# Reordering engine instructions in the first two wide attention pairs of a fused attention and ELU-FFN kernel

## The chip, the cores and the metric

The kernel runs on one core of a Trainium2 chip. The metric is the time of one execution on the device in microseconds (us). Before the change it is 1258.76 us, the median of 3 runs (1257.75 to 1259.64).

## The reference

Two blocks follow each other. The attention block keeps only scores close to the row maximum; the second block is a two-layer FFN with an ELU between the layers. Everything is float32.

```python
# q, k, v: (8, 8, 576, 64), batch x heads x sequence x head size; tau = 0.02
scores = 1/sqrt(64) * q @ k.transpose(0, 1, 3, 2)
thresh = max(scores, axis=-1) - tau
scores = where(scores >= thresh, scores, -1e9)
attn = exp(scores - max(scores)); attn = attn / (sum(attn) + 1e-9)
x = (attn @ v).transpose(0, 2, 1, 3).reshape(4608, 512)
h = x @ w_in                                   # (512, 2048)
g = where(h > 0, h, exp(min(h, 0)) - 1)
out = g @ w_out                                # (2048, 512)
```

## The kernel before, in words

Attention goes by pairs of heads, 32 in all, numbered from 0. A pair has four square query steps (128 queries of both heads) and one tail step (the last 64 queries of both). A step is: score matmuls into PSUM, a row maximum on VectorE (DVE), an exponential on ScalarE (ACT), a mask with row sums on DVE, a scaling on GpSimd (POOL) or ACT, and a turn: DVE transposes 32x32 blocks into a tile `x` (`turn_squares`, L868 and L877), SyncE (SP) stores `x` to DRAM (`there`, L881 for a tail step, L893 for a square one), and a later DMA brings it back turned. There are two buffers of `x`, so a turn can begin only when the stores of the turn before the last one have landed.

From pair 9 on (`JOINED`) the pairs are wide: two square steps share five PSUM banks. `tail_step` issues the tail scores of the own pair and the value matmuls of an older pair, `wide_step` the scores of two square steps, and between them TensorE (PE) gets quarters of FFN work: Strassen products of the first layer (`first_product`) and of the second (`second_round`). One `first_product` has seven quarters, which go through three PSUM banks in turn:

- quarter 0 ends in an ACT copy `w1`, 1 in an ACT copy `u2` and a POOL addition `u2 += w1`, 2 in an ACT copy `s1` and a POOL subtraction `s1 -= u2` (copies L1692, POOL L1697);
- quarters 3 and 4 end in an ACT copy into the hidden tile `g` (L1739, L1740), 4 also in a POOL subtraction `t5` (L1697);
- quarters 5 and 6 end in a DVE addition out of PSUM into `g` (L1700, with operand `t5` or `s1`), and then in an ELU: ACT exponential (L1708), minus one on ACT (L1720) or POOL (L1718), DVE combination (L1728).

The bank of a quarter is free for a quarter of the next product once its copy or addition has been done.

Every engine runs its own instructions in order. The order is planned on the host: `at(t, f, key)` puts a job on an agenda with due time `t` plus an offset `MOVED[stage + key]`, and jobs are issued by due time whenever the planned PE clock passes them. The stage is `j` in pair 9 and `s` or `f` in later pairs, so an offset whose name begins with `j` acts in pair 9 alone. The key `5.0` is job 0 behind quarter 5 of the pair (28 quarters, four products); `max30` is the maximum of step 3, head 0; `exp30`, `exp31` are its exponentials; `turn4` is the turn of the tail step; `w0` stores 512 KB of weight sums to DRAM (L2097).

```python
        def at(t, f, key=None):
            if key and stage[0]:
                t += MOVED.get(stage[0] + key, 0.0)
```

Accesses to the five wide banks go through `on_banks`: any engine's access to a bank waits for all earlier accesses of other engines to that bank, reads included. An exponential of step 3 thus waits for a maximum issued before it on a shared bank.

In `tail_step` of pair 10, the values of pair 8 are copied out of PSUM by ACT (`values_out`, L1060 and L1066) in a job that was due at the end of the value matmuls.

Of the kernel before, what the change touches and what calls it, by code (L numbers as in the profile page):

```python
# [368 lines left out]
def kernel(  # L369
# [545 lines left out]
    def values(pr, part, pv=None):  # L915
        b, j = divmod(pr, NPAIR)
        vm, vd = (raws[pr][x] for x in ("vm", "vd"))
        wT = wTs.pop((pr, part))
        if b not in xts:
            xts[b] = xpool.tile([P, KJ, MAIN], FP32, name="xt")  # L920
        n = wT.shape[1] * T
        if pv is None:
            pv = psum["t"].tile([P, 512], FP32, name="pv", tag="rt")
        watch = on_banks if wide else lambda *a: None
        watch(nc.tensor.matmul(pv[:, :n], vd, wT[:, :, NC], start=True, stop=False, skip_group_check=True), pv[:, :n])
        for c in range(NC):
            for h in range(2):
                g0, g1 = (2 * h, 2 * h + 10) if part else (0, 2 * NT)
                o = pv[h * D : (h + 1) * D, g0 * T : g1 * T]
                watch(nc.tensor.matmul(o, vm[:, h, c], wT[:, g0:g1, h * (NC + 1) + c], start=False, stop=(c == NC - 1),  # L930
                                       skip_group_check=True), o)
        return lambda: values_out(pr, part, pv)
# [49 lines left out]
    def wide_max(pr, i, h):  # L982
        st = open_steps[pr, i]
        on_banks(nc.vector.tensor_reduce(st["mx"][:, h : h + 1], st["sc", h], axis=AX.XY if i == NC else AX.X, op=ALU.max,  # L984
                                         negate=True),
                 st["sc", h])

    def wide_bounds(pr, i):
        st, hs = open_steps[pr, i], heads_of(i)
        sunk = [(pr, i, h) in WIDE_ACT for h in hs]  # L990
        for h in hs[:1] if len(set(sunk)) == 1 else hs:
            cs = slice(0, len(hs)) if len(set(sunk)) == 1 else slice(h, h + 1)
            if sunk[h]:
                nc.gpsimd.tensor_scalar(st["th"][:, cs], st["mx"][:, cs], ntau, None, ALU.subtract)
            else:
                nc.gpsimd.tensor_scalar(st["th"][:, cs], st["mx"][:, cs], -1.0, ntau, ALU.mult, ALU.add)  # L996

    def wide_exp(pr, i, h):
        st = open_steps[pr, i]
        if (pr, i, h) in WIDE_ACT:  # L1000
            on_banks(nc.scalar.activation(st["e", h], st["sc", h], AF.Prelu, bias=st["th"][:, h : h + 1], scale=1.0, alpha=STEEP),
                     st["sc", h])
        else:
            on_banks(nc.scalar.activation(st["e", h], st["sc", h], AF.Exp, bias=st["mx"][:, h : h + 1]), st["sc", h])  # L1004

    def wide_mask(pr, i, h):
        st = open_steps[pr, i]
        if (pr, i, h) in WIDE_ACT:
            nc.scalar.activation(st["e", h], st["e", h], AF.Exp, bias=ntau, accum_out=st["sm"][:, h, :1])
            return  # L1010
        on_banks(nc.vector.scalar_tensor_tensor(st["e", h], st["sc", h], st["th"][:, h : h + 1], st["e", h], ALU.is_ge,  # L1011
                                                ALU.mult, accum_out=st["sm"][:, h, :1]), st["sc", h])
# [602 lines left out]
    with tc.manual_schedule():  # L1615
# [14 lines left out]
            serial[0] += 1  # L1630
            heapq.heappush(agenda, (t, serial[0], f))
# [9 lines left out]
        def on_pe(cost, f):  # L1641
            until(clock[0])
            f()
            clock[0] += cost
            return clock[0]
# [261 lines left out]
        def finish_of(pr, i, t_sum, t_turn):  # L1907
            at(t_sum, lambda: reciprocal_of(pr, i, heads_of(i)), f"sum{i}")
            for h in heads_of(i):
                at(t_sum + 0.25 + 0.75 * h, lambda h=h: (normalize_act if (pr, i, h) in WIDE_NORM else normalize_pool)(pr, i, h), f"norm{i}{h}")  # L1910
            at(t_turn, lambda: turn_squares(pr, i), f"turn{i}")
# [6 lines left out]
        def tail_step(pr):  # L1918
            t, v = clock[0], pr - 2
            own, joined = pr if pr < NP else None, v if v >= JOINED else None  # L1920
            loc = {}
            on_pe(1.2, lambda: loc.update(zip(("main", "outs"), tails_and_values(own, joined))))
            if pr == JOINED:
                end = on_pe(2.5, lambda: loc.update(out=values(JOINED - 1, 0, wide[0][:, 2 * 512 : 3 * 512])))
                at(end - 2.0, lambda: loc["out"]())
            if own is not None:
                at(t + 1.25, lambda: wide_max(pr, NC, 0), "max4")
                at(t + 2.0, lambda: wide_bounds(pr, NC), "bound4")
                at(t + 2.0, lambda: wide_exp(pr, NC, 0), "exp4")
                at(t + 3.3, lambda: wide_mask(pr, NC, 0), "mask4")  # L1930
                finish_of(pr, NC, t + 4.2, t + 10.5)
            if joined is not None:
                for part, cost in ((1, 2.2), (0, 1.8)):
                    end = on_pe(cost, lambda: loc["main"](part))
                    at(end, loc["outs"][part], f"out{part}")
            elif v == JOINED - 1:
                end = on_pe(3.0, lambda: loc.update(out=values(v, 1, wide[0][:, 2 * 512 : 3 * 512])))
                at(end, lambda: loc["out"]())

        def wide_step(pr, half):  # L1940
            t = clock[0]
# [145 lines left out]
        for pr in range(JOINED, NP + 2):  # L2087
# [17 lines left out]
            if JOINED < pr < NP:  # L2105
                at(t + 7.0, lambda pr=pr: load(pr, ("v",)), "v" if stage[0] == "j" else None)
            tail_step(pr)
            v_end = clock[0]
            if pr % NPAIR == 1 and pr < NP + 1:
# [139 lines left out]
        end = middle + UNIT * NFT  # L2249
# [102 lines left out]
```

## Time and profile before

| | |
|---|---|
| median of 3 runs | 1258.76 us |
| the profiled execution | 1259.32 us |
| its span, first to last instruction | 1257.5 us |
| PE busy | 1243.9 us (99%) |
| DVE busy | 1040.3 us (83%) |
| POOL busy | 727.1 us (58%) |
| ACT busy | 635.2 us (51%) |
| DMA queue of SP | 72.2% of 16 engines' span |
| TensorE clock granted | 1.000 |

Pair 9 stands in the span from 259 to 293 us, the tail step of pair 10 from 293 to 300.5 us. In the timeline a row has its start in us, its length in us, the engine, the line, the operation, output and inputs, the shapes and a count; in brackets the idle time of the engine before it and what ended that.

### The profile page before, as it was taken

How to read it: one execution, taken by the hardware profiler on the slowest of the kernel's cores; microseconds unless marked ns; L12 is line 12 of the kernel's file. 1: busy time of each engine (PE TensorE's matmuls, PEld its weight loads, DVE VectorE, ACT ScalarE, POOL GpSimd, SP SyncE). 2: the span in 40 equal slices, each digit the busy share in tenths (PEclk: the TensorE clock that was granted, in tenths of full speed). 3: DMA queues.
4: the chain of work that ended last, by engine and by line, in shares of the span. 5: the costliest groups of instructions: out<-in, count | busy, mean ns of one | idle time of the engine just before them, and what ended most of it. 6: DMA issues, size and time to landing. Idle time of an engine off the chain costs nothing.

```text
span 1257.5 us, 21116 instructions
## 1 busy us (share of the span) xinstructions
PE 1243.9 (99%) x6598; PEld 957.0 (76%) x6598; DVE 1040.3 (83%) x2199; ACT 635.2 (51%) x1331; POOL 727.1 (58%) x1061
## 2 busy tenths in 40 slices
PE   8999999999999999999999999999999999999998
PEld 6676576467878787888778787878788887788886
DVE  7888778789798988898889879898889876776983
ACT  7989776664352526253534435252625353465330
POOL 4778655687475847666576747584766655122000
PEclk9999999999999999999999999999999999999999
DMA  7557688998889898998989998999889885000001
GB/s 134 151 177 177 177 244 234 260 248 216 239 239 266 245 240 224 241 263 228 252 206 253 237 231 231 256 257 240 228 238 262 221 241 175 20 1 1 1 34 34
DMA packets 325551, 245.74 MB, mean 195 GB/s; under 512 B 209216, under 2 KB 289984, under 8 KB 325440
## 3 DMA queue, kind: packets, MB, share of 16 engines
q1 hardware_dynamic: 323264, 243.65, 72.2%
q8 instruction: 52, 0.85, 0.3%
q10 hardware_dynamic: 2176, 0.75, 0.2%
q14 instruction: 59, 0.48, 0.1%
HBM read 154.53 MB, written 89.78 MB: 194 GB/s over the span
## 4 chain that ended last, share of the span: by engine, by line
PE 90%; DVE 3%; DMA 2%; ACT 2%; issue 1%; SPq 1%; POOL 1%; DVEq 0%; ACTq 0%; POOLq 0%
PE f L1678 23%; PE f L1818 22%; PE sc L977 8%; PE sc L1050 7%; PE f L2278 7%; PE f L2203 5%; PE f L1102 4%; PE sc L673 3%; PE f L1154 3%; PE f L2216 2%; PE pv L930 2%; PE rt L792 1%; PE sc L1042 1%; PE sc L1037 1%; DMA there<-x 1%
## 5 line engine op out<-in xcount | busy, mean ns | idle before, releaser
L984 DVE TENSOR_REDUCE mx<-sc 128x1 f32<-128x576 f32 x207 | 148.3, 750 | 28.5 <-PE sc L977 24.6
L726 POOL TENSOR_SCALAR w<-w,rs 128x576 f32<-128x576 f32 x144 | 115.8, 813 | 70.0 <-DVE rs L789 69.8
L1004 ACT ACTIVATE w<-sc,mx 128x576 f32<-128x576 f32 x113 | 81.5, 740 | 116.0 <-DVE mx L984 98.7
L868 DVE STREAM_TRANSPOSE x<-w 128x512 f32<-128x512 f32 (+1 forms) x153 | 108.9, 744 | 15.3 <-POOL w L726 11.3
L996 POOL TENSOR_SCALAR th<-mx,ntau 128x2 f32<-128x2 f32 (+1 forms) x114 | 33.8, 297 | 133.3 <-DVE mx L984 133.3
L977 PE MATMUL sc<-kT,qT 64*128 64x448 f32 (+4 forms) x736 | 103.4, 416 | 0.2 <-ACT xs L1066 0.2
L977 PEld LDWEIGHTS sc<-kT,qT 64*128 64x128 f32 x736 | 81.0, 186 | 25.1 <-issue 16.5
L1011 DVE SCALAR_TENSOR_TENSOR w<-sc,th,w 128x576 f32<-128x576 f32 x113 | 88.2, 811 | 9.4 <-ACT w L1004 9.2
L1678 PE MATMUL f<-xt,sw 128*128 128x256 f32 x384 | 93.8, 386 | 1.8 <-DVE g L1700 1.8
L1678 PE MATMUL f<-xt,w_in 128*128 128x256 f32 x384 | 92.2, 382 | 0.0
L1818 PE MATMUL f<-w_out,s 128*128 128x256 f32 x384 | 92.0, 382 | 0.1
L1818 PE MATMUL f<-w_out,g 128*128 128x256 f32 x384 | 92.0, 382 | 0.0
L1678 PE MATMUL f<-x,w_in 128*128 128x256 f32 x384 | 90.9, 379 | 0.0
L1818 PE MATMUL f<-t,s 128*128 128x256 f32 x384 | 90.8, 379 | 0.0
L726 POOL TENSOR_SCALAR e<-e,rs 128x576 f32<-128x576 f32 x91 | 67.1, 741 | 35.6 <-DVE rs L789 34.2
L1678 PEld LDWEIGHTS f<-xt,sw 128*128 128x128 f32 x384 | 69.4, 189 | 18.6 <-issue 4.8
L1678 PEld LDWEIGHTS f<-xt,w_in 128*128 128x128 f32 x384 | 71.7, 190 | 12.7 <-ACT w L1692 2.2
L1818 PEld LDWEIGHTS f<-w_out,g 128*128 128x128 f32 x384 | 72.0, 190 | 12.4 <-issue 3.1
L1818 PEld LDWEIGHTS f<-w_out,s 128*128 128x128 f32 x384 | 71.9, 190 | 12.4 <-issue 2.5
L1678 PEld LDWEIGHTS f<-x,w_in 128*128 128x128 f32 x384 | 72.8, 190 | 10.5 <-ACT s L1692 0.6
L1818 PEld LDWEIGHTS f<-t,s 128*128 128x128 f32 x384 | 72.8, 190 | 10.3 <-POOL s L1765 0.4
L1765 POOL TENSOR_TENSOR s<-g 128x256 f32<-128x256 f32 x96 | 74.9, 785 | 7.9 <-DVE g L1728 7.5
(316 smaller groups left out, 3103.5 us busy)
## 6 DMA issues: line engine op xcount, KB each, us to landing
there<-x SPq DMA_DIRECT2D x444, 144.0 KB, 3.5
wTb<-there SPq DMA_DIRECT2D x58, 576.0 KB, 6.5
wTa<-there SPq DMA_DIRECT2D x53, 576.0 KB, 5.0
sw<-win_sums SPq DMA_DIRECT2D x46, 384.0 KB, 4.9
t<-wout_sums SPq DMA_DIRECT2D x33, 512.0 KB, 6.2
qm<-in_q_dram SPq DMA_DIRECT2D x124, 72.0 KB, 4.9
wst<-in_moe_w_in_dram SPq DMA_DIRECT2D x16, 512.0 KB, 4.4
vm<-in_v_dram SPq DMA_DIRECT2D x64, 128.0 KB, 3.9
```

The lines of the kernel that those rows point to most:

```text
L726: nc.gpsimd.tensor_scalar(wv, wv, st["rs"][:, h : h + 1], 1.0, ALU.mult, ALU.mult)
L868: nc.vector.transpose(x[:, :, c0 : c0 + nc_], src.rearrange("p (c g n) -> p g c n", c=nc_, n=T))
L977: on_banks(nc.tensor.matmul(o, qT[r, i * P : (i + 1) * P], kT[r, k0 : k0 + n], start=True, stop=True, skip_group_check=True), o)
L984: on_banks(nc.vector.tensor_reduce(st["mx"][:, h : h + 1], st["sc", h], axis=AX.XY if i == NC else AX.X, op=ALU.max, negate=True), st["sc" ...
L1004: on_banks(nc.scalar.activation(st["e", h], st["sc", h], AF.Exp, bias=st["mx"][:, h : h + 1]), st["sc", h])
L1011: on_banks(nc.vector.scalar_tensor_tensor(st["e", h], st["sc", h], st["th"][:, h : h + 1], st["e", h], ALU.is_ge, ALU.mult, accum_out=st[" ...
L1050: on_banks(nc.tensor.matmul(o, vm[:, h, c], parts[part][:, g0:g1, h * (NC + 1) + c], start=False, stop=(c == NC - 1), skip_group_check=Tru ...
L1678: nc.tensor.matmul(loc["banks"][place], left[:, j], right[:, j], start=(begins and j == 0), stop=(j == 1), skip_group_check=True)
L1765: engine.tensor_tensor(o, x, y, op)
L1818: nc.tensor.matmul(place(m), lhs, rhs, start=(begins and v == 0), stop=(v == RU - 1), skip_group_check=True)
L2203: nc.tensor.matmul(o, w.rearrange("p (j f) -> p j f", j=KJ)[:, j], m, start=(j == 0 and x == 0), stop=(j == KJ - 1 and x == 1), skip_group ...
L2278: nc.tensor.matmul(banks8[2 * i + x // 2], h[:, tok], w, start=(f == 0 and x != 1), stop=(f == NFT - 1 and x != 0), skip_group_check=True)
```

## The change

Eight offsets and one due time change. No instruction is added or taken away; only the order on the engines is another. By the planned due times of the program:

- `turn4` goes from 10.84 to 12.44: on DVE it comes behind the additions of quarters 5 and 6 (11.07, 11.39) and the maximum `max10` (12.21); on SP its four stores come behind `w0` (11.90).
- `15.1` (`u2 += w1`) goes from 21.80 to 21.30, on POOL ahead of the thresholds of step 2 (21.58); `16.1` (`s1 -= u2`) goes from 23.17 to 24.37, so that `t5` of quarter 18 (23.78) comes ahead of it.
- `max30` goes from 23.54 to 25.44, on DVE behind the additions of quarters 19 and 20; `exp31` (24.20 to 25.60) and `exp30` (24.85 to 25.75) follow it as before. `19.0` goes from 25.16 to 24.76.
- `19.1` (an ELU's exponential) goes from 26.41 to 27.31, on ACT behind the copy `u2` of quarter 22.
- The copies of pair 8's values in pair 10's tail step are due 2.0 earlier, on ACT ahead of the exponential of pair 10's tail (`exp4`).

```diff
-    "j14.0": -3.68, "j15.0": -1.62, "j15.1": -0.67, "j16.0": 0.04, "j16.1": -0.22, "j16.2": 0.31, "j17.0": -2.16,
-    "j18.0": -0.97, "j19.0": -0.84, "j19.1": -0.29, "j18.1": -1.3, "j2.0": -4.57, "j2.1": 0.76, "j2.2": 0.93, "j20.0": -4.05, "j20.1":
+    "j14.0": -3.68, "j15.0": -1.62, "j15.1": -1.17, "j16.0": 0.04, "j16.1": 0.98, "j16.2": 0.31, "j17.0": -2.16,
+    "j18.0": -0.97, "j19.0": -1.24, "j19.1": 0.61, "j18.1": -1.3, "j2.0": -4.57, "j2.1": 0.76, "j2.2": 0.93, "j20.0": -4.05, "j20.1":
...
     "jexp00": -0.08, "jexp01": -0.52, "jexp10": -0.11, "jexp11": 0.42, "jexp20": -0.3, "jexp21": 0.68, "jexp30":
-    -0.93, "jexp31": -0.68, "jexp4": 0.88, "jfetch0": 2.01, "jfetch1": 4.84, "jloadk": -2.59, "jloadq": -4.91, "jm00":
+    -0.03, "jexp31": 0.72, "jexp4": 0.88, "jfetch0": 2.01, "jfetch1": 4.84, "jloadk": -2.59, "jloadq": -4.91, "jm00":
...
-    0.48, "jmax30": 1.11, "jmax31": 0.34, "jmax4": -9.77, "jnorm00": 0.93, "jnorm01": 0.48, "jnorm10": 0.12,
+    0.48, "jmax30": 3.01, "jmax31": 0.34, "jmax4": -9.77, "jnorm00": 0.93, "jnorm01": 0.48, "jnorm10": 0.12,
...
-    0.07, "jsum4": -0.37, "jturn0": -1.09, "jturn1": -0.06, "jturn2": 2.17, "jturn3": 0.29, "jturn4": -2.27, "jw0":
+    0.07, "jsum4": -0.37, "jturn0": -1.09, "jturn1": -0.06, "jturn2": 2.17, "jturn3": 0.29, "jturn4": -0.67, "jw0":
...
             elif v == JOINED - 1:
                 end = on_pe(3.0, lambda: loc.update(out=values(v, 1, wide[0][:, 2 * 512 : 3 * 512])))
-                at(end, lambda: loc["out"]())
+                at(end - 2.0, lambda: loc["out"]())
```

## The prediction, made before the changed kernel was run

> **What bounds the kernel now.** I read the page first, then the idle time of PE stretch by stretch, then the timelines of DVE, SP and ACT where PE idles.
>
> ```profile
> PE 1243.9 (99%) x6598; PEld 957.0 (76%) x6598; DVE 1040.3 (83%) x2199; ACT 635.2 (51%) x1331; POOL 727.1 (58%) x1061
> ```
>
> PE is the bound: 13.6 us of the span are idle. From 301 us on its timeline shows no wait that is not repeated in every pair, so a microsecond won or lost by then is won or lost at the end. The waits within reach stand in PE's own timeline:
>
> ```profile
> 268.93 1.03 PE L1678 MATMUL f<-xt,sw 128*128 128x256 f32 x4
> 271.32 1.13 PE L1678 MATMUL f<-xt,sw 128*128 128x256 f32 x4 [1.37 <-DVE g L1700]
> ...
> 287.23 1.13 PE L1678 MATMUL f<-xt,sw 128*128 128x256 f32 x4 [0.44 <-DVE g L1700]
> ...
> 297.14 1.02 PE L977 MATMUL sc<-kT,qT 64*128 64x448 f32 x2
> 298.40 2.17 PE L977 MATMUL sc<-kT,qT 64*128 64x320 f32 x14 [0.25 <-ACT xs L1066]
> ```
>
> Quarters follow each other at 0.87 us (two take 1.73 at 267.20 to 268.93). By that pitch the first wait costs 1.53 us, the second 0.61, the third about 0.6. All else between 263 and 301 us is 0.2 or less. These are what the change goes for; at most some 2.8 us can come back.
>
> **The first wait: additions ahead of the tail's turn.** DVE's timeline:
>
> ```profile
> 265.82 1.42 DVE L984 TENSOR_REDUCE mx<-sc 128x1 f32<-128x576 f32 x2
> 269.86 0.71 DVE L868 STREAM_TRANSPOSE x<-w 128x512 f32<-128x512 f32 x1 [2.62 <-DMA there<-x]
> 270.49 0.46 DVE L877 STREAM_TRANSPOSE x<-w 128x128 f32<-128x128 f32 x2
> 270.88 0.39 DVE L1700 TENSOR_TENSOR g<-f,t 128x256 f32<-128x256 f32 x1
> 271.19 0.41 DVE L1700 TENSOR_TENSOR g<-f,s 128x256 f32<-128x256 f32 x1
> ```
>
> DVE stands idle for 2.62 us at the tail's turn, for its tile `x`, and both additions queue behind it. Put ahead, the first can start when POOL's `t` ends (267.89 + 0.74 = 268.63), the second when quarter 6 ends (269.09). PE's next quarter then starts at 269.8, not 271.32: 1.53 us sooner. `max10` fills the gap too, to 270.2; the turn (1.02) follows, and `max11` starts at 271.24 instead of 272.19. So DVE leads by 0.95 us. PE keeps no more than that: the next wide scores need the bank that mask L1011 reads until 276.93, and PE issued them at 277.00. PE's 1.53 shrink to 0.95 there, and ACT and POOL, which wait on DVE in this stretch, move along.
>
> **What that move drags along: the turn's stores.** SP issues without a gap here:
>
> ```profile
> 273.68 0.65 SPq L901 DMA_DIRECT2D wTb<-there  x1
> 274.43 1.88 SPq L881 DMA_DIRECT2D there<-x  x4
> 276.40 0.96 SPq L2097 DMA_DIRECT2D wout_sums<-t  x2
> ```
>
> The four stores (L881, 80 KB each) now stand behind `w0`, the first L2097, 512 KB. The last store was issued at 275.84 and landed 4.6 us later, at 280.4; the two L2097 were issued at 276.40 and 276.90 and landed 5.6 and 6.2 later, at 282.0 and 283.1. The queue is backed up, DMA is busy all the time (share 1.03 to 1.07, 384 to 409 GB/s in 278 to 282 us), and landings come in the order of issue. 524 KB at 409 GB/s are 1.3 us: the stores land at about 281.65. Bounds: the issue slot alone, 0.45 us (280.85), or the whole landing step of `w0`, 1.57 us (281.95). I take 1.25, nearest to the bytes. Who waits: the second square turn (L868 at 281.04) reuses that buffer of `x`. Before, it had 0.65 us in hand; now DVE comes to it at 280.1 and waits until 281.65 + 0.12 (the latency seen at 269.86, landing 269.74) = 281.77. The lead of 0.95 becomes a lag of 0.73 (bounds: a lead of 0.07, a lag of 1.04). All of DVE is queued behind that turn: two maxima, two ELUs, a mask, the next additions.
>
> The Trainium skill ("DMA: Bandwidth & Descriptors", Queues, rings and completion order) says that each engine takes descriptors in ring order but that completion is not FIFO per issuing engine. In this window all landings are in the order of issue, so the trace bears out its first half alone; by the second the stores could land at the old time, which is a rival below.
>
> **The second wait: additions ahead of `max30`.** Before, DVE ran mask 285.36, `max30` 286.09, additions 286.76 and 287.10. Now the additions come first: with a lag of 0.73 the mask is at 286.09, the first addition at 286.82 to 287.23, and PE's quarter starts at 287.3, where it was (287.23). The gain of 0.67 just pays the lag. The two POOL moves make this possible: `t` ended at 286.71, 0.05 before its addition; with `u2` ahead of the thresholds and `t` ahead of `s` it ends by 285.9. They cost nothing by themselves, as POOL idled 1.71 us before the threshold at 283.92. `max30` pays: it ends at 286.84 + 0.73 + 0.67 = 288.24, 1.40 later. Behind it ACT has an unbroken run:
>
> ```profile
> 286.88 1.38 ACT L1004 ACTIVATE w<-sc,mx 128x576 f32<-128x576 f32 x2 [0.65 <-DVE mx L984]
> 288.14 0.37 ACT L1692 COPY w<-f 128x256 f32<-128x256 f32 x1
> 288.39 0.65 ACT L1708 ACTIVATE ge<-g 128x512 f32<-128x512 f32 x1
> 289.07 0.64 ACT L1720 ACTIVATE ge<-ge 128x512 f32<-128x512 f32 x1
> 289.62 0.35 ACT L1692 COPY u<-f 128x256 f32<-128x256 f32 x1
> 289.86 0.78 ACT L714 ACTIVATE e<-e,rs 128x576 f32<-128x576 f32 x1
> 290.54 0.36 ACT L1692 COPY s<-f 128x256 f32<-128x256 f32 x1
> ```
>
> From the end of `max30` (286.84) to the end of the last copy (290.90) are 4.06 us without a gap, and PE's quarter of 290.98 waits for that copy. Nothing in it is shortened: copy `u` ahead of the exponential only swaps two of its members, and the 0.1 us that PE waited for `u` at 290.02 is no longer the later wait. So that quarter starts at 288.24 + 4.06 + 0.08 = 292.38, **1.40 us late**. DVE's masks wait for the same exponentials and lag by 1.35: from there on all engines are late alike.
>
> **The third wait: copies ahead of the tail's exponential.** ACT ran minus (to 297.05), exponential 296.96 to 297.68, copies 297.58 to 298.26. PE's values end at 297.21. With the copies first they run 297.25 to 297.93, and PE's second score pair starts 0.33 sooner. But the exponential ends 0.92 later, at 298.60; the mask on DVE starts at 298.65 instead of 297.95, holding its bank until 299.46 instead of 298.76; and PE's third group writes that bank. It started at 299.02 and cannot before 299.5. Behind the waiting mask stands an ELU that nobody needs by then. **Loss 0.5 us** (bounds: a gain of 0.33 if the bank were free, a loss of 0.7 if the mask's delay passes in full).
>
> **Sum.** 1.40 + 0.5 = 1.9 us later. Against the profiled execution, 1259.32 (span 1257.5 and 1.8 around it), that is 1261.2; the median of the runs lies 0.56 lower, so 1258.76 + 1.9 = 1260.7. With both terms at their ends: 0.60 - 0.33 = +0.3, and 1.71 + 0.7 = +2.4. About 0.2% (2.5 us) is what a measurement of this kernel can tell from no change, so this is "within".
>
> **Rivals.**
> *No wait for the stores:* they land by 280.0. For: the buffer had 0.65 us in hand. Against: a full queue, ordered landings. DVE keeps its lead: `max30` 0.28 sooner, less 0.5: +0.2, 1259.0.
> *Faster:* PE is the bound and gets its waits back, because ACT's run behind `max30` gives way (its exponentials wait on that maximum only by a shared bank) and the stores land in time. 1.53 + 0.61 + 0.6 = 2.7 less: 1256.0. For: PE at 99%. Against: the bracket at 286.88 names the maximum, and DVE has next to no gap from 269.86 to 295.8. It decides only if `max30` ends before 285.3.
> *Slower:* DVE and POOL block each other behind the late turn. An ELU (L1728) took 0.69 at 282.47 and 1.03 at 284.41, beside POOL additions (L1697) of 0.72 and 1.06. Now that ELU is due at 281.77 + 1.43 + 0.61 + 0.66 + 0.67 = 285.14 (turn, ELU, two maxima), and `t` starts on POOL at 285.1 (first maximum to 284.56, two thresholds of 0.27): 0.35 more if DVE loses, and again 0.35 if the subtraction behind it delays the second addition. With both, 1.9 + 0.7 = 2.6: 1261.4. It decides if `t` starts first.
> The Trainium skill ("SBUF — State Buffer", SBUF: two separate sides) calls this an exclusive lock held for the whole instruction; the pair at 284.41 agrees. By it the ELU would wait out `t` in full, which is the 0.35.
> *The change doesn't do what it says:* due times decide the order, and they cross as listed; negligible.
>
> **Chances.** Forecast 0.46, a quarter of it above 2.5 us; slower 0.26; no wait 0.17; faster 0.11, nearly all beyond 0.2%. So faster 0.10, within 0.52, slower 0.38. The range takes in the rival without the wait, with the runs' scatter of about 0.9 below it, and the slower rival with 0.7 above: 1258.1 to 1262.1, leaving out the faster rival and a little above.
>
> **What would show it.** DVE: additions near 268.7 and 269.1, `max11` near 271.2; idle time of some 1.7 us before the second square turn, ended by DMA `there<-x`, and that turn near 281.8: if it starts at 280.1, the step on the stores is wrong. PE: no wait at 269.8, one of about 1.8 us ended by DVE L1700 near 287.3, another ended by ACT near 292.4, and the third score group behind mask L1011. If PE's first L1818 comes before 300.5, I am wrong in sign.

## The result, and the profile after

The changed kernel takes 1262.13 us (median of 10 runs, 1261.07 to 1262.93) beside 1258.70 for the kernel before (10 runs on the same chip, 1257.18 to 1260.49). The ratio is 1.0027 with a 95% interval of 1.0017 to 1.0036: about 3.4 us slower. The forecast of 1260.7 is 1.4 too low, its range ends 0.03 below the median, and the median lies outside its likeliest case, "within 0.2%". The sign was right.

The profiled execution took 1262.34 us with a span of 1260.6. The page's line of busy times hardly differs from that of before (PE 1243.9):

```profile
PE 1245.4 (99%) x6598; PEld 957.2 (76%) x6598; DVE 1040.0 (83%) x2199; ACT 634.8 (50%) x1331; POOL 726.8 (58%) x1061
```

Busy time doesn't show a change of order; the timeline does. All rows of pair 9 lie 0.2 us later in this trace than in that of before, because its first tail scores (L1037) start at 259.18 and not at 258.98. DVE's timeline after the change, with one row of POOL:

```profile
268.86 0.42 DVE L1700 TENSOR_TENSOR g<-f,t 128x256 f32<-128x256 f32 x1 [1.42 <-POOL t L1697]
269.32 0.42 DVE L1700 TENSOR_TENSOR g<-f,s 128x256 f32<-128x256 f32 x1
269.67 0.75 DVE L984 TENSOR_REDUCE mx<-sc 128x1 f32<-128x576 f32 x1
270.33 0.70 DVE L868 STREAM_TRANSPOSE x<-w 128x512 f32<-128x512 f32 x1
...
279.50 0.74 DVE L984 TENSOR_REDUCE mx<-sc 128x1 f32<-128x576 f32 x1
281.59 1.44 DVE L868 STREAM_TRANSPOSE x<-w 128x640 f32<-128x640 f32 x2 [1.35 <-ACT ge L1720]
...
284.60 0.72 POOL L1697 TENSOR_TENSOR t<-g,u 128x256 f32<-128x256 f32 x1
284.85 1.02 DVE L1728 SCALAR_TENSOR_TENSOR g<-ge,g 128x512 f32<-128x512 f32 x1
...
286.53 0.41 DVE L1700 TENSOR_TENSOR g<-f,t 128x256 f32<-128x256 f32 x1
286.87 0.41 DVE L1700 TENSOR_TENSOR g<-f,s 128x256 f32<-128x256 f32 x1
287.20 0.74 DVE L984 TENSOR_REDUCE mx<-sc 128x1 f32<-128x576 f32 x1
```

The 2.62 us wait at the tail's turn is gone, the additions stand ahead of it, and a new wait of 1.35 us stands before the second square turn. The profile names an ACT instruction as what ended it. SP's timeline says what else ended then:

```profile
273.39 0.38 SPq L2097 DMA_DIRECT2D wout_sums<-t  x1
273.87 2.82 SPq L881 DMA_DIRECT2D there<-x  x4
```

The store `w0` now stands ahead of the four stores of the turn; the last of those landed at 281.47, and the turn started 0.12 later, the same latency as in the trace of before. PE's timeline:

```profile
269.12 1.89 PE L1678 MATMUL f<-xt,sw 128*128 128x256 f32 x8
...
287.00 1.13 PE L1678 MATMUL f<-xt,sw 128*128 128x256 f32 x4 [1.09 <-DVE g L1700]
...
289.66 1.99 PE L1678 MATMUL f<-xt,w_in 128*128 128x256 f32 x8 [0.67 <-ACT w L1692]
292.05 1.99 PE L1678 MATMUL f<-x,w_in 128*128 128x256 f32 x8 [0.39 <-ACT s L1692]
...
300.81 1.67 PE L977 MATMUL sc<-kT,qT 64*128 64x256 f32 x12 [0.84 <-DVE w L1011]
302.40 0.91 PE L1818 MATMUL f<-w_out,g 128*128 128x256 f32 x3
```

No wait is left at 269, and four stand behind it that were not there or were shorter. I call the time from the first tail scores of pair 9 to the first L1818 the **stretch**: 41.53 us before, 43.22 after (259.18 to 302.40). Before, it begins and ends with these rows:

```profile
258.98 1.19 PE L1037 MATMUL sc<-kT,qT 64*64 64x288 f32 x8
...
300.51 1.78 PE L1818 MATMUL f<-w_out,g 128*128 128x256 f32 x7
```

These 1.69 us are what the forecast put at 1.9. Behind the stretch come 957.02 us before and 958.16 after; one new wait is visible there, a wait for `sw`, the weight sums of the first layer, which L1250 loads for each product:

```profile
834.93 1.32 PE L1678 MATMUL f<-xt,sw 128*128 128x256 f32 x5 [0.52 <-DMA sw<-win_sums]
```

PE falls back by 0.67 us at that wait. Another 0.4 come at some 705 us in steps that show no wait. So the two profiled executions differ by 3.02 us: 0.20 ahead of the stretch, 1.69 in it, 1.14 behind it. Which of these hold for the medians is what the experiments had to find out.

### The profile page after: what moved, and what is told of

Its sections match the earlier page's. It is cut to its first block, busy times and chain, and to the rows that moved or that the text cites. A ratio compares the mean times of both kernels' runs of the same rounds, so it can differ in the third digit from the quotient of the medians.

```text
span 1260.6 us, 21116 instructions
## 1 busy us (share of the span) xinstructions
PE 1245.4 (99%) x6598; PEld 957.2 (76%) x6598; DVE 1040.0 (83%) x2199; ACT 634.8 (50%) x1331; POOL 726.8 (58%) x1061
## 4 chain that ended last, share of the span: by engine, by line
PE 91%; DVE 3%; ACT 2%; DMA 2%; issue 1%; POOL 1%; SPq 0%; DVEq 0%; ACTq 0%; POOLq 0%
PE f L1818 23%; PE f L1678 22%; PE sc L977 8%; PE sc L1050 7%; PE f L2278 7%; PE f L2203 5%; PE f L1102 4%; PE sc L673 3%; PE f L1154 3%; PE f L2216 2%; PE pv L930 2%; PE rt L792 2%; PE sc L1042 1%; PE sc L1037 1%; DMA there<-x 1%
## 5 line engine op out<-in xcount | busy, mean ns | idle before, releaser
L868 DVE STREAM_TRANSPOSE x<-w 128x512 f32<-128x512 f32 (+1 forms) x153 | 108.9, 744 | 14.0 <-POOL w L726 11.2
L977 PE MATMUL sc<-kT,qT 64*128 64x448 f32 (+3 forms) x736 | 103.7, 417 | 0.8 <-DVE w L1011 0.8
L1011 DVE SCALAR_TENSOR_TENSOR w<-sc,th,w 128x576 f32<-128x576 f32 x113 | 88.2, 810 | 11.0 <-ACT w L1004 10.8
L1818 PE MATMUL f<-w_out,s 128*128 128x256 f32 x384 | 92.0, 382 | 0.1
L1818 PE MATMUL f<-w_out,g 128*128 128x256 f32 x384 | 92.0, 382 | 0.0
L1818 PE MATMUL f<-t,s 128*128 128x256 f32 x384 | 90.8, 379 | 0.0
L1818 PEld LDWEIGHTS f<-w_out,g 128*128 128x128 f32 x384 | 72.0, 190 | 12.4 <-issue 3.1
L1818 PEld LDWEIGHTS f<-w_out,s 128*128 128x128 f32 x384 | 71.9, 190 | 12.5 <-issue 2.5
L1818 PEld LDWEIGHTS f<-t,s 128*128 128x128 f32 x384 | 72.8, 190 | 10.3 <-POOL s L1765 0.4
```

The source lines that it names most:

```text
L868: nc.vector.transpose(x[:, :, c0 : c0 + nc_], src.rearrange("p (c g n) -> p g c n", c=nc_, n=T))
L977: on_banks(nc.tensor.matmul(o, qT[r, i * P : (i + 1) * P], kT[r, k0 : k0 + n], start=True, stop=True, skip_group_check=True), o)
L1818: nc.tensor.matmul(place(m), lhs, rhs, start=(begins and v == 0), stop=(v == RU - 1), skip_group_check=True)
```

## The experiments

Each kernel was timed beside the kernel before on the same chip; there the kernel before had medians of 1258.57, 1258.99 and 1258.21 us in the three sets. "Landing" is that of the last of the four stores L881, counted from the start of the stretch: 21.41 before, 22.28 after.

**e1_turn: the turn alone, on the kernel before.**

```diff
-"jturn4": -2.27
+"jturn4": -0.67
```

> The kernel before with one edit: the tail's turn of pair 9 later, as in the change (its four stores then stand behind the 512 KB store w0). The measure is the stretch from PE's first tail score of pair 9 (L1037) to PE's first second-layer product of pair 10 (L1818): 41.53 us before, 43.22 in the changed kernel. Theory S (the stores behind w0 hold up the next square turn): DVE waits over 1 us for DMA there<-x before the second square turn, which starts near 281.6; the stretch is 41.9 to 42.2, longer than before although PE's first wait of 1.5 us is gone. Rival V (the loss comes from the order on DVE and ACT alone, max30 and the copies): without these moves the lead of 0.95 us is kept, no idle DVE before that turn, stretch 40.6. The whole time: S 1259.0 to 1259.5, V 1257.8.

1261.37 us, ratio 1.0022 (1.0013 to 1.0031). The profiled execution was one of the longest of its 11: 1263.96 us. Its stretch is 44.29, even longer than with the whole change; stretch and median are both beyond what either theory had. The stores landed at 23.70 in this execution:

```profile
282.75 1.44 DVE L868 STREAM_TRANSPOSE x<-w 128x640 f32<-128x640 f32 x2 [2.76 <-DMA there<-x]
```

Here the profile names the store. The direction speaks for theory S; the size was off, as the landing spreads by more than I had thought. PE's wait of 2.78 us behind it did one thing more, told in the last section.

**e2_all_w0: the whole change, but `w0` behind the four stores again.**

```diff
 (the changed kernel)
-"jw0": 2.29
+"jw0": 2.99
```

> The changed kernel with one edit: w0 due 0.7 later, so that the four stores of the tail's turn stand ahead of it again, as in the kernel before. Theory S: they land near 280.2 to 280.4, the second square turn starts by 280.6, and the stretch is 1.1 us shorter than the changed kernel's: 42.0 to 42.2 (still over 41.53: max30's delay and the copies ahead of the exponential remain). Rival V: the stores do not matter, stretch 43.2. A second rival R (the DMA queue is as full as before and DVE waits all the same, for another store): turn near 281.5, stretch 43.0.

1261.32 us, 1.0020 (1.0011 to 1.0029), stretch 42.80. A miss: theory S had 42.0 to 42.2. The stores still landed at 21.84 and DVE still waited 0.90; the turn at 281.53 and this stretch are nearest to rival R (281.5 and 43.0), but the store waited for is the same as before: the turn started 0.12 behind its landing. The stretch is 0.42 shorter than after the change, for a landing 0.44 earlier.

**e3_all_but_out: the whole change without the copies ahead of the tail's exponential.**

```diff
 (the changed kernel)
-                at(end - 2.0, lambda: loc["out"]())
+                at(end, lambda: loc["out"]())
```

> The changed kernel with one edit undone: the copies of pair 8's values behind the tail's exponential again. If these copies cost 0.5 us (prediction), the stretch is 42.6 to 42.8 and PE's wait for mask L1011 in pair 10's score group (0.84 us in the changed kernel) is gone, a wait for the copies (ACT xs L1066, some 0.2 to 0.3) back. Rival: the copies are paid by the lag that is there anyway; stretch 43.2. Second rival: they cost the whole delay of the exponential, 0.9; stretch 42.3.

1260.96 us, 1.0019 (1.0011 to 1.0028), stretch 42.37 with a landing of 22.46: nearest to the second rival (42.3), which had the copies cost the whole delay of the exponential. PE's wait for mask L1011 is gone, and no wait for the copies is back. ACT and then DVE in this kernel:

```profile
297.24 0.61 ACT L1720 ACTIVATE ge<-ge 128x512 f32<-128x512 f32 x1
297.76 0.72 ACT L1004 ACTIVATE w<-sc,mx 128x576 f32<-128x576 f32 x1
298.38 0.36 ACT L1060 COPY xt<-sc 128x256 f32<-128x256 f32 x1
```

```profile
298.76 0.80 DVE L1011 SCALAR_TENSOR_TENSOR w<-sc,th,w 128x576 f32<-128x576 f32 x1
```

and in the changed kernel:

```profile
297.31 0.61 ACT L1720 ACTIVATE ge<-ge 128x512 f32<-128x512 f32 x1
298.36 0.37 ACT L1060 COPY xt<-sc 128x256 f32<-128x256 f32 x1 [0.43 <-PE sc L930]
298.62 0.42 ACT L1066 COPY xs<-sc 64x64 f32<-64x64 f32 x2
299.07 0.74 ACT L1004 ACTIVATE w<-sc,mx 128x576 f32<-128x576 f32 x1
```

```profile
299.93 0.82 DVE L1011 SCALAR_TENSOR_TENSOR w<-sc,th,w 128x576 f32<-128x576 f32 x1 [1.02 <-ACT w L1004]
```

In its place behind the exponential, the copy waits for nothing and starts at the same time (298.38) as ahead of it (298.36), where it waits 0.43 for PE's values. The move wins nothing and delays the exponential by 1.31 and the mask by 1.17.

**e4_turn_w0: additions first, but with the four stores still ahead of `w0`, on the kernel before.**

```diff
-"jturn4": -2.27
+"jturn4": -0.67
-"jw0": 2.29
+"jw0": 2.99
```

> The kernel before with two edits: the tail's turn later as in the change, and w0 behind its stores. Nothing else of the change. Theory S: the stores land as before, the lead of DVE is cut to some 0.5 to 0.7 us by the landing, and the stretch is 40.8 to 41.0; whole time 1258.1. Rival V': the wait at the turn is not from w0; DVE idles 1 us and the stretch is 41.9 as with the turn alone.

The second square turn waits for nothing and PE's second wait is short:

```profile
280.30 1.42 DVE L868 STREAM_TRANSPOSE x<-w 128x640 f32<-128x640 f32 x2
```

```profile
286.48 1.13 PE L1678 MATMUL f<-xt,sw 128*128 128x256 f32 x4 [0.44 <-DVE g L1700]
```

The stretch is 40.45, 1.08 shorter than in the profile of before, and its profiled execution took 1258.61. But the median is 1259.72, ratio 1.0010 (1.0000 to 1.0019). The 11 times fall in two groups, four of 1258.11 to 1258.61 and seven of 1259.57 to 1263.78; the profile is of the first, and none shows what the others lost. In the whole change too the median lost some 1.7 us more than the stretch shows. My guess was the waits for `sw`.

**n0_before_held, n1_after_held, n4_turn_w0_held: no late loads of `sw`.** The same edit on the kernel before, on the changed kernel and on e4_turn_w0. It leaves out loads, so these kernels compute another result and serve for their times alone:

```diff
+        held = {}
...
             if x < len(first_order):
-                load_in(first_order[x][1])
+                if x < 6:
+                    load_in(first_order[x][1])
+                    held[x % 2] = in_sums[first_order[x][1]]
+                else:
+                    in_sums[first_order[x][1]] = held[x % 2]
```

> The kernel before, but the weight sums of the first layer (tile sw, loads of L1250) are loaded only up to the sixth product; from the seventh on (349 us) the two tiles then in SBUF are used again, so later products are formed with the wrong weight sums and 42 of 46 loads are left out. It is the base for the next two runs. The stretch from the first tail scores of pair 9 to the first L1818 of pair 10 stays at 41.5 us. Theory S (the timed runs lose time to late sw loads, at random per execution, and the changed kernels more of it than the kernel before): 1257.0 to 1258.7. Theory R (those loads cost nothing and the excess is elsewhere): 1258.6, within 0.3.

> The changed kernel with the same loads left out from the seventh product on. Stretch 43.2, and no wait of PE for sw from 349 us on. Theory S (the change loses 1.7 us in the stretch, the rest of its 3.4 us in waits for late sw loads): the difference to n0_before_held comes down to 1.5 to 2.0 us, in the medians too. Theory R (the excess behind the stretch has another cause): the difference stays at 3.0 to 3.7 us.

> e4_turn_w0 (the kernel before with turn4 behind the two additions, and w0 behind the four stores of the turn) with the same loads left out. Its stretch was 40.45, 1.1 us shorter than before, yet it was 1.1 us slower in the median. Theory S: it is 0.9 to 1.3 us faster than n0_before_held. Theory R: it stays 0.5 to 1.5 us slower than n0_before_held.

Medians of 1258.72, 1262.36 and 1258.55. The changed kernel is 3.64 slower than n0_before_held, its base without those loads, as theory R had it (3.0 to 3.7), so theory S falls for it: the waits for `sw` are not where the loss of its median is. For e4_turn_w0 neither theory's range came. Without the loads it ties with n0_before_held (1258.55 beside 1258.72; ratio to the kernel before 0.9996, 0.9988 to 1.0005, where e4_turn_w0 had 1.0010) with the same stretch (40.49), so the waits for `sw` may be part of its loss; its one profile shows none.

The surprise is n0_before_held's stretch. The edit touches nothing before 349 us, and yet it was 39.62 and not 41.53: the wait of 2.62 us at the tail's turn was not there. In the profile of before the last of the four square stores (L893) that this turn waits for landed at 269.74, in n0_before_held at 267.59. The packets suggest why. A view of the DMA of before, 267.75 to 269.2 us:

```profile
DMA packets 97, 0.40 MB, mean 276 GB/s; under 512 B 4, under 2 KB 12, under 8 KB 97
```

Eight of these (12 under 2 KB less 4 under 512 bytes) are packets of 1152 bytes, the last eight of the 128 of that store. They start one after the other from 268.41 on, just as a packet of another queue ends (268.43), a 16 KB instruction fetch of 1.25 us. It stands in the view of 267.1 to 268.4:

```profile
q8 instruction: 1, 0.02, 6.0%
```

Eight is a sixteenth of 128, the share of one of 16 DMA engines. In e5_out, below, the same: the fetch ended at 268.18, the last eight began at 268.17, landing 269.44. In n0_before_held the fetch came at 267.27, when the last of the store's packets had already started (267.15).

**e12_stores_first: the square stores out of the fetch's way.** Two stores of finished data (L1067, L1143) that stood ahead of the four L893 on SP go behind the next four:

```diff
+    puts, put = [], lambda f: (puts.append(f), f() if len(puts) not in (11, 12) else None)
...
-            nc.sync.dma_start(xtail[j, :, b * TAIL : (b + 1) * TAIL], xs)
+            put(lambda: nc.sync.dma_start(xtail[j, :, b * TAIL : (b + 1) * TAIL], xs))
...
-            nc.sync.dma_start(out[g * S + t0 : g * S + t0 + P, :], ot)
+            put(lambda: nc.sync.dma_start(out[g * S + t0 : g * S + t0 + P, :], ot))
...
-        at(0.0, lambda: turn_squares(JOINED - 1, NB - 1))
+        at(0.0, lambda: (turn_squares(JOINED - 1, NB - 1), [f() for f in puts[10:12]]))
```

> The kernel before, with two stores (L1067, L1143) taken out of SP's queue ahead of the four stores of the square turn that the tail's turn waits for, and put behind the next four. Theory C: those stores' wait is a matter of chance. In the profile of before the last eight packets of the fourth store began when a 16 KB instruction fetch ended (268.43), the store landed at 269.74 and DVE waited 2.62 us; in n0_before_held they were through before the fetch, the store landed at 267.59, DVE hardly waited and the stretch was 39.62 instead of 41.53. Two issue slots earlier (about 1.0 us) the stores are out of the fetch's way in every execution: landing below 267.3, stretch 39.4 to 40.0, and a median of 1257.2 to 1257.9. Rival D (the landing is late by the queue's state, and moves with the queue alone): landing about 1.0 us sooner, wait and stretch spread as before, median 1258.0 to 1258.8.

The stores landed at 266.45 and the first wait is gone, as theory C had it. The time is not: 1258.51 us, ratio 1.0002 (0.9993 to 1.0011), stretch 40.43 where 39.4 to 40.0 was expected. DVE's timeline:

```profile
267.89 0.71 DVE L868 STREAM_TRANSPOSE x<-w 128x512 f32<-128x512 f32 x1 [0.47 <-POOL w L726]
...
268.91 0.38 DVE L1700 TENSOR_TENSOR g<-f,t 128x256 f32<-128x256 f32 x1
...
280.23 1.44 DVE L868 STREAM_TRANSPOSE x<-w 128x640 f32<-128x640 f32 x2 [0.99 <-POOL ge L1718]
```

DVE has the turn done by the time the operand of the first addition is there (POOL's `t` ends at 268.81), comes early to the second square turn, and waits there for the stores instead (landed 280.11, turn 0.12 behind). The median is as rival D had it (1258.0 to 1258.8), the landing as theory C.

**b_again and a_again: both kernels once more, unchanged, for a second profile.**

> The kernel before, unchanged, for a second profile. Theory C: either as in the first (fourth store landing near 269.6, wait of DVE over 2 us at the tail's turn, stretch 41.3 to 41.7, some 1259.3 us) or as in n0_before_held (landing near 267.6, hardly a wait, stretch 39.5 to 40.0, some 1257.4 us). Rival: in between, with a wait that grows evenly.

> The changed kernel, unchanged, for a second profile. The four profiles with the changed turn, the store w0 ahead of the turn's four and the copies show the stretch as the landing of the last of those stores, counted from the first tail scores of pair 9, plus 20.95 us (43.22 for 22.28, 42.80 for 21.84, 43.83 for 22.88). So here too: landing 21.8 to 23.8, stretch 42.7 to 44.8, second square turn 0.12 behind the landing. Theory L (the executions' typical landing is later than in the first profile, which is why the median lost 3.4 and not 1.9): landing over 22.8. Rival: landing 22.3 or less, and the time is lost behind the stretch.

b_again took 1258.97 us, and it is neither of the two cases expected. The square stores landed early (8.49 after the start of the stretch, not 10.75), and the wait stands where it stands in e12_stores_first:

```profile
267.90 0.71 DVE L868 STREAM_TRANSPOSE x<-w 128x512 f32<-128x512 f32 x1 [0.48 <-POOL w L726]
...
280.79 1.44 DVE L868 STREAM_TRANSPOSE x<-w 128x640 f32<-128x640 f32 x2 [1.54 <-POOL ge L1718]
```

Stretch 40.98 with a landing of 21.49. a_again took 1261.86, with a landing of 22.46, between the two cases expected, and a stretch of 43.39; it has no wait for `sw` behind the stretch, and names the DMA:

```profile
282.07 1.44 DVE L868 STREAM_TRANSPOSE x<-w 128x640 f32<-128x640 f32 x2 [1.52 <-DMA there<-x]
```

**e5_out and e6_max30: the copies alone, and the moves around `max30` alone, on the kernel before.**

```diff
 (e5_out)
-                at(end, lambda: loc["out"]())
+                at(end - 2.0, lambda: loc["out"]())
 (e6_max30)
-"j15.1": -0.67  "j16.1": -0.22  "j19.0": -0.84  "j19.1": -0.29  "jexp30": -0.93  "jexp31": -0.68  "jmax30": 1.11
+"j15.1": -1.17  "j16.1":  0.98  "j19.0": -1.24  "j19.1":  0.61  "jexp30": -0.03  "jexp31":  0.72  "jmax30": 3.01
```

> The kernel before with the copies of pair 8's values due 2.0 us sooner, and nothing else. The prediction's term: 0.5 us later in the stretch (42.0; bounds 41.2 to 42.2), by way of the exponential and the mask L1011 whose bank the third score group of the tail writes. By the difference of the profiles of the changed kernel with and without this edit it is 0.85 (42.4). Theory S: the time follows with 1259.1 to 1260.0, and some waits for sw on top. Rival: PE's second score pair gains 0.33 and the bank is free in time: 41.2.

> The kernel before with the moves around max30 alone: max30, exp30, exp31, 19.0, 19.1 and the two operands on POOL; the turn and the copies stay. By the prediction's steps this part gains 0.67 at the second wait and pays 1.40 by the later maximum where the turn's lag is there; without the lag 0.67 later at max30: stretch 0.4 to 0.8 longer than before for the same wait at the tail's turn (41.9 to 42.3 with the long one, 40.0 to 40.4 without it), and 0.3 to 0.8 us slower in the median. Rival, by the profiles of the turn alone and of all but the copies (44.29 and 42.37, with landings of 23.70 and 22.46): counted from the landing this part makes the stretch 0.68 shorter, so 0.4 to 0.7 faster.

e5_out: 1259.84 us, ratio 1.0007 (0.9998 to 1.0016), stretch 42.19 with a landing of 21.90, between the two sizes expected (42.0 and 42.4). e6_max30: 1259.17, 1.0003 (0.9994 to 1.0012; the two medians alone give 1.0008), stretch 41.67 with a landing of 21.36. Neither can be told from no change in the times alone; the stretches, taken against the landing, can:

| order of instructions | landing | stretch | difference |
|---|---|---|---|
| before: n0_before_held, e12_stores_first, b_again | 20.12, 20.94, 21.49 | 39.62, 40.43, 40.98 | 19.50, 19.49, 19.49 |
| moves around `max30`: e6_max30 | 21.36 | 41.67 | 20.31 |
| the copies: e5_out | 21.90 | 42.19 | 20.28 |
| all but the copies: e3_all_but_out | 22.46 | 42.37 | 19.91 |
| whole change: after, a_again, n1_after_held, e2_all_w0 | 22.28, 22.46, 22.88, 21.84 | 43.22, 43.39, 43.83, 42.80 | 20.94, 20.93, 20.95, 20.96 |

Wherever the second square turn starts as soon as the stores have landed (0.12 to 0.13 us behind, in all these profiles), the stretch is that landing plus a number that belongs to the order: the same within 0.02 us over three profiles of one order and within 0.03 over four of another. Outside the table stand the first profile of before, e4_turn_w0 and n4_turn_w0_held, where that turn waited for nothing, and e1_turn (20.59), with its lower clock.

Against the 19.49 of before, the moves around `max30` cost 0.82 and the copies alone 0.79. The rival for e6_max30, a gain of 0.68, falls.

No version here beats the kernel before by more than its interval.

## Why the prediction was right in its mechanism and too small

**The additions ahead of the turn: right.** They ran at 268.86 and 269.32 (268.7 and 269.1 predicted), PE lost its wait there, and `max11` started at 271.34 (271.2). The trace after lies 0.2 us later as a whole; where one of its times is set against a predicted one below, that is taken off.

**The stores behind `w0`: right in place, too large for this profile.** Landing 281.27 for 281.65, so 0.87 later than before and not 1.25; turn 281.39 for 281.77, DVE's wait 1.35 for 1.7, PE's wait near 287 only 1.09 for 1.8. The rival without that wait falls with a_again, where the profile names the store and the turn stands 0.12 behind its landing. Over all 14 profiles the landing goes by this order: 22.28 to 23.70 in the five with `w0` ahead of the four stores (after, a_again, n1_after_held, e3_all_but_out, e1_turn), 20.06 to 21.90 in the nine with `w0` behind. Putting `w0` back in the changed kernel (e2_all_w0) left a landing of 21.84 and a wait of 0.90, though: the issue order of two transfers is only part of what sets the landing.

The Trainium skill ("DMA: Bandwidth & Descriptors", Queues, rings and completion order) says that completion is not FIFO per issuing engine. In all 14 profiles the 56 to 63 transfers that SP issued between 255 and 300 us landed in the order of issue without an exception (eight semaphores tell the landings; two transfers on the same one are told apart by their order alone, and have seven others between them), so no run here shows that half of the rule.

**`max30` behind the additions: right.** It ended at 287.74 (288.24), and PE's quarter behind ACT's run came at 291.85 (292.38). Not foreseen: one quarter sooner PE waits 0.67 for the copy `w` of the same run (the row at 289.66), so the loss is spread over two waits. The step priced the move itself at 0.67 (the two additions put ahead); e6_max30 measures 0.82.

**The copies: the sign right, the size not.** 0.5 was predicted, 0.7 at most. a_again and e3_all_but_out have the same landing (22.46) and differ by this edit: 1.02 us. On the kernel before (e5_out) the same edit costs 0.79. The working took ACT's minus to end about when PE's values do, as before. After the change ACT is ahead: its minus ends at 297.92, the values at about 298.3, and the exponential, which could have run in between, waits for both copies.

**The sum: near for the stretch of the two profiles, partly by luck, and too small for the medians.** 1.9 was predicted, 1.69 came in the stretch: up to PE's quarter behind ACT's run 0.87 for 1.40, from there to the first L1818 0.82 for 0.5. The two errors cancel in part. For the medians the step that failed is the last one, "the median of the runs lies 0.56 lower, so 1258.76 + 1.9": it took the profiled execution of before as a typical one with a constant off it. In it, DVE waited 2.62 us at the tail's turn and so came to the second square turn 0.65 after the stores had landed. The second square turn in the first profile of before, in n0_before_held and in e5_out (where the profile names an ACT instruction, and the stores had landed at 280.87):

```profile
281.04 1.42 DVE L868 STREAM_TRANSPOSE x<-w 128x640 f32<-128x640 f32 x2
```

```profile
279.19 1.44 DVE L868 STREAM_TRANSPOSE x<-w 128x640 f32<-128x640 f32 x2 [0.15 <-DMA there<-x]
```

```profile
280.99 1.44 DVE L868 STREAM_TRANSPOSE x<-w 128x640 f32<-128x640 f32 x2 [0.18 <-ACT ge L1708]
```

In b_again, e12_stores_first and n0_before_held the first wait is 0.51 or less and the second is 1.54, 0.99 and 0.15; in e6_max30 they are 0.78 and 0.48, in e5_out 2.34 and 0.18. So with the tail's turn in its old place the second square turn waited for the same stores already in five of six profiles, and the one that the forecast was built on is the exception. The two waits hide each other: taking the first away wins little (e12_stores_first: 1.0002), and the lead of 0.95 us that the forecast counted against the stores' delay does not exist where the turn waits for them already.

Against that base the terms are other ones: landing 1.53 later (means of 22.54 for after, a_again and n1_after_held, and 21.01 for before, b_again and n0_before_held), `max30` 0.82, copies 1.03 (20.94 less 19.91), and 0.40 given back by the additions ahead of the turn (19.91 less 20.31): 2.98. The terms are those of one order of adding the edits; the copies alone cost 0.79, so they don't add up in every order. The mean stretches of the same six profiles are 43.48 and 40.71, 2.77 apart, because in the first profile of before the stretch was 0.62 longer than its landing asks.

The medians are 3.43 apart. The same six executions are 3.42 apart in their whole mean times: 0.18 ahead of the stretch, where the two kernels are the same, 2.77 in it and 0.47 behind it, most of that in the one profile with a wait for `sw` (after: 1.14 more than before, a_again 0.15). That those waits make up the rest in the medians is not shown, and n1_after_held, which loses 3.64 without them, speaks against it as a general answer. The rest of 0.5 to 0.7 is not settled; three profiles of each kernel don't fix a mean landing that ranges over 1.4 us in one order.

**The rivals.** *Slower by DVE and POOL blocking each other:* its condition came, as `t` started on POOL at 284.60 and the ELU on DVE at 284.85. But the ELU took 1.02 us, as long as the one at 284.41 before (1.03), which had stood beside the addition `u`: the 0.35 was in the base already, and nothing was added. Nor does waiting out `t` in full give 0.35: by the prediction's own times, `t` (0.72) started 0.04 ahead of the ELU. The slower time came by another way. *Faster:* it needed `max30` to end before 285.3, and it ended at 287.74. The remark that nothing behind 301 us has slack to lose was too strong by the `sw` loads.

## What to carry to other kernels

A wait in one profile is worth its removal only if nothing else stands ready behind it: ask, for the consumer it delays, what it would wait for next if it came early, and look at a second profile of the same kernel before counting a wait that a DMA ends. Where a stretch ends with a transfer, measure every edit against that transfer's landing: that turned stretches which scatter by over 1 us within one order into terms that repeat to 0.03. And a copy moved ahead of an exponential on an engine in order wins only if its input is there first.

## What the runs showed of the hardware that was not expected

An instruction fetch seems able to hold up one sixteenth of a store: a 16 KB packet of 1.25 us, and the store's last eight packets began 0.01 to 0.02 before its end by the records. The landing came some 2 us late in these two of the 13 profiles with the square stores in the old order: 10.75 and 10.47 us after the start of the stretch, 8.36 to 8.91 in the others. A fetch beside the store does not always do it: in e1_turn one stood from 266.86 to 269.35, and the store's last packet began at 267.36. The records don't name the DMA engine of a packet, so that fetch and packets shared one is inferred from the coincidence in both.

A wait of PE of 2.78 us was followed by a lower clock. The windows of e1_turn, with PE's busy time, that of the other engines, the granted clock, DMA share and GB/s:

```profile
284.00:286.00 2.00, 2.00 (x10) 1.47 (x8) 2.00 (x4) 0.00 (x0) 0.48 (x2) 1.00 1.01 372
286.00:288.80 2.80, 0.04 (x1) 0.00 (x0) 2.80 (x7) 1.93 (x4) 2.47 (x5) 1.00 1.10 356
288.80:290.50 1.70, 1.67 (x4) 1.32 (x5) 1.67 (x5) 1.70 (x4) 1.56 (x4) 0.58 1.17 152
290.50:292.20 1.70, 1.70 (x5) 1.35 (x4) 1.63 (x7) 1.67 (x4) 1.42 (x3) 0.50 0.70 230
```

From 289.1 on the granted clock was 0.5 for 3.41 us. After the waits of 1.09 to 1.69 us that the other profiles have in the stretch it stayed at 1.0. The length of a wait does not decide alone, though. Near the start every profile has a PE wait of 1.12 us that ends at 9.4 to 10.2 us; in a_again, b_again and e12_stores_first the clock was 0.5 for 3.41 us from 11.2 to 11.4 us on, in the other 11 it was not. The Trainium skill ("TensorE: Matmul & The Clock Gate", HAM oscillation — how this bites in real kernels) gives gaps of over about 3.4 us as what to avoid; here the lower clock followed a gap of 2.78, and the 3.41 us agree with the length of its window.
